# A state-space and feed-forward block: the first 512 tokens normalised and transposed in two halves, three tiles of gate and up matmuls at 256 columns

## The chip, the core and the metric

The kernel runs on one core of a Trainium2 chip. The time is device microseconds for one execution, the median of several runs; lower is better. TensorE does the matmuls, VectorE the elementwise work, ScalarE the activation functions and part of the copies out of PSUM, GpSimd a few small operations, and SyncE issues most DMAs. PSUM has eight banks of 128 x 512 fp32 here.

## The reference

The input x is 2048 tokens of 512 channels. It is normalised without weights, and two branches run on the result: a diagonal complex state-space layer with 512 states, and a gated feed-forward layer with 1376 hidden columns. The output is x plus both.

```python
xn = _layernorm(x, axis=-1)
# A: Lam_bar = exp(dt * Lam);  Bu = xn @ B_bar^T
#    h_t = Lam_bar * h_(t-1) + Bu_t;  y = 2 * Re(h @ C^T) + xn * Dskip
# B: (gelu(xn @ w_gate) * (xn @ w_up)) @ w_down
return x + A(xn) + B(xn)
```

Types are bf16, with fp32 sums in PSUM.

## The kernel before

The tokens are cut into four blocks of 512. Each block is normalised (LN), transposed so that channels lie on partitions (TR), and then used by three kinds of matmuls: gate and up (GU, 11 tiles of 128 hidden columns, the last of 96), the input of the state-space layer (BU), and the down and output matmuls of both branches into one bank (DN). Between BU and DN, VectorE turns the complex recurrence into real scans (CHAIN: multiplications with cosine and sine tables around 8 scans).

No engine's order is written by hand. Every operation is recorded with an engine, a function, an assumed duration and the buffers that it reads and writes (`S.op`, `S.dma`). `schedule` then walks through a model of the chip: TensorE and SyncE keep the order in which operations were recorded; VectorE, ScalarE and GpSimd take, of the operations whose inputs are recorded, the one with the earliest due time (worked back from the TensorE operation that needs it) if it can start within 150 ns of the earliest start, and otherwise fill the gap with work that fits. `emit` writes each engine's list in that order, with semaphore waits for what the buffers require. So the assumed durations decide the order, and the order is fixed when the chip runs. The planner knows no activation tables; the compiler puts a table load ahead of any ScalarE function that the loaded table does not hold.

The steps at the start, with their lines:

- Four DMAs load x of block 0, one per 128 tokens (L425). Three vectors of parameters (log_dt, Lambda_re, Lambda_im) follow on SyncE's queue (L409), then the first chunks of the gate and up weights (L421), Dskip, x of block 1 (L415), and so on. Weights come in three chunks of hidden columns, 0 to 512, 512 to 1024 and 1024 to 1376.
- 16 warm matmuls of 512 columns (L769) multiply the identity with the first x tile. Their result is not used.
- LN(0) on VectorE: statistics per 128 tokens (L563), aggregates (L564), casts and the addition of epsilon (L565 to L568). GpSimd takes the square root as a power of 0.5 (L569), VectorE the reciprocal (L570). Subtraction of the mean (L575) and multiplication (L583 on VectorE, L587 on ScalarE) are two operations per 128 tokens, with the buffer D1 between them.
- TR(0) on TensorE: two groups of eight 128 x 128 transposes (L609), each copied out of PSUM by ScalarE (L620) or VectorE (L616). Blocks 1 to 3 are transposed by DMA (L596) instead.
- GU(0): per tile, four matmuls for gate and four for up (L686) into two banks; ScalarE applies Gelu to the one (L690) and copies the other (L694); VectorE multiplies them (L696). Banks are dealt out in turn, eight of them (`next_bank`).
- The state-space parameters: Exp of log_dt (L482), Exp of its product with Lambda_re (L485), Sin (L493), a score of tiny VectorE operations (L483 to L510), and twelve diagonal matrices (L514). All Gelus wait for this Sin (`GATE`). Between GU(0)'s tiles from tile 4 on, prepB (L533, copied by L538) multiplies B with the diagonals.

In the later stages BU is L633 (copied by L637), DN is L730 and its result is added to x by L742.

Of the kernel before, what the change touches and what calls it, by code (L numbers as in the profile page):

```python
# [73 lines left out]
class Sched:  # L74
# [61 lines left out]
    def schedule(self, pe_start=12000.0):  # L136
# [40 lines left out]
        while nleft:  # L177
# [35 lines left out]
            if op.kind == "dma":  # L213
                free_at[e] = st + 60.0
                xfer = op.dur - 2000.0
                t0 = max(st, dma_pipe)
                dma_pipe = t0 + xfer
                op.finish = t0 + xfer + 2000.0
            else:
                op.finish = st + op.dur  # L220
                free_at[e] = op.finish
# [92 lines left out]
def build(nc, ins, out, dbg=None, stage=99, opts=None):  # L314
    dbg = dbg or {}
    opts = opts or {}
    with ExitStack() as es:
        E = es.enter_context
        S = Sched(nc, es)
        S.fence_slack = float(opts.get("fence_slack", FENCE_SLACK))  # L320
# [12 lines left out]
        FCH = [(0, 512), (512, 1024), (1024, F)]  # L333
# [9 lines left out]
        D1_all = A.alloc("D1", [4, D], BF16); D1 = ring(D1_all, "D1", 4)  # L343
# [13 lines left out]
        MB = A.alloc("MB", [NB, 4], BF16)  # L357
        NEGM = A.alloc("NEGM", [NB, 4], F32)
# [5 lines left out]
        blk = lambda buf, b, nm: A.sub(buf, "%s_%d" % (nm, b), b)  # L364
        MBb = [blk(MB, b, "MB") for b in range(NB)]; NEGMb = [blk(NEGM, b, "NEGM") for b in range(NB)]
        VBb = [blk(VB, b, "VB") for b in range(NB)]; SBQb = [blk(SBQ, b, "SBQ") for b in range(NB)]
        QBb = [blk(QB, b, "QB") for b in range(NB)]; RQb = [blk(RQ, b, "RQ") for b in range(NB)]
# [34 lines left out]
        if "DN" in dbg:  # L402
            DNB = A.alloc("DNB", [4, D], F32)
# [8 lines left out]
        do_ssm = stage >= 3  # L412

# [5 lines left out]
        def ld_w(W, Wc, src, ci):  # L419
            f0, f1 = FCH[ci]  # L420
            return S.dma(lambda e: e.dma_start(W.ap[:, :, f0:f1], src[:, f0:f1].rearrange("(k p) f -> p k f", p=128)),  # L421
                         512 * (f1 - f0) * 2, writes=[Wc[ci]], tag="ld_w")
# [3 lines left out]
        if do_ssm:  # L426
            for T_, nm in ((LDT, "A_log_dt"), (LRE, "A_Lambda_re"), (LIM, "A_Lambda_im")):
                S.dma(ld_param(T_, ins[nm]), 1024, writes=[T_], tag="ld_" + nm)
# [4 lines left out]
        if do_ssm:  # L433
            for c, nm in enumerate(("A_B_re", "A_B_im")):
                S.dma(lambda e, c=c, nm=nm: e.dma_start(BN.ap[:, c], ins[nm].rearrange("(s p) d -> p s d", p=128)),
                      512 * 1024, writes=[A.sub(BN, "BN%d" % c, c)], tag="ld_" + nm)
# [8 lines left out]
        XT_DMA = opts.get("xt_dma", (1, 2, 3))  # L445

        def load_CT():
            CTc = [A.sub(CT_all, "CTc%d" % c, c) for c in range(2)]
            for c, nm in enumerate(("A_C_re", "A_C_im")):
                S.dma(lambda e, c=c, nm=nm: e.dma_start_transpose(CTc[c].ap, ins[nm]),  # L450
                      opts.get("ct_bytes", 2.0) * 512 * 1024, writes=[CTc[c]], tag="tr_" + nm, fenced=True)
        wchunk = lambda ft: 0 if ft < 4 else (1 if ft < 8 else 2)
# [5 lines left out]

        V(lambda e: e.memset(HALF.ap, 0.5), D_TINY, [], [HALF], "half")
        POOL(lambda e: e.iota(IOT.ap, [[1, 128]], base=0, channel_multiplier=-1), 300, [], [IOT], "iota")  # L460
        V(lambda e: e.tensor_scalar(IDN.ap, IOT.ap, 0.0, None, ALU.is_equal), d_dve_ts4x(128), [IOT], [IDN], "ident")
        if do_ssm:
            POOL(lambda e: e.iota(IOTJ.ap, [[1, 512]], base=0, channel_multiplier=0), 600, [], [IOTJ], "iotj")
# [13 lines left out]
        last_table_op = None  # L477
        GATE = {"before_gelu": []}
        if do_ssm:
            (A_, TH, RRr, LBR, LBI, N1, TAa, TBb, DEN, RDEN, TC, TD, NRE, TE, TF, NIM, CR, CI) = range(18)  # L480
            pa = lambda i: PA[i].ap
            t1 = ACT(lambda e: e.activation(DTB.ap, LDT.ap, ACTF.Exp), d_act(4), [LDT], [DTB], "exp_dt")  # L482
            V(lambda e: e.tensor_tensor(pa(A_), DTB.ap, LRE.ap, ALU.mult), D_TINY, [DTB, LRE], [PA[A_]])  # L483
            V(lambda e: e.tensor_tensor(pa(TH), DTB.ap, LIM.ap, ALU.mult), D_TINY, [DTB, LIM], [PA[TH]])
            t2 = ACT(lambda e: e.activation(pa(RRr), pa(A_), ACTF.Exp), d_act(4), [PA[A_]], [PA[RRr]], "exp_a", after=[t1])  # L485
            w16 = lambda a, b_: W16.ap[:, a:b_]
            W16p = [A.sub(A.alloc("W16v", [4, 4], F32, at=W16.lo), "W16_%d" % i, i) for i in range(4)]
            V(lambda e: e.tensor_scalar(w16(0, 4), pa(TH), 1.0 / TWO_PI, None, ALU.mult), D_TINY, [PA[TH]], [W16p[0]])
            V(lambda e: e.tensor_scalar(w16(4, 8), pa(TH), 512.0 / TWO_PI, None, ALU.mult), D_TINY, [PA[TH]], [W16p[1]])
            V(lambda e: e.tensor_scalar(w16(8, 16), w16(0, 8), 0.25, None, ALU.add), D_TINY, W16p[0:2], W16p[2:4])  # L490
            V(lambda e: e.tensor_copy(KI.ap, W16.ap), D_TINY, W16p, [KI])
            V(lambda e: e.tensor_tensor(FRC.ap, W16.ap, KI.ap, ALU.subtract), D_TINY, W16p + [KI], [FRC])
            t3 = ACT(lambda e: e.activation(SC16.ap, FRC.ap, ACTF.Sin, scale=SIN_SCALE), d_act(16), [FRC], [SC16], "sin16", after=[t2])  # L493
            GATE = {"before_gelu": [t3]}
            sinT, sinP, cosT, cosP = (SC16.ap[:, 4 * i:4 * i + 4] for i in range(4))
            V(lambda e: e.tensor_tensor(pa(LBR), pa(RRr), cosT, ALU.mult), D_TINY, [PA[RRr], SC16], [PA[LBR]])
            V(lambda e: e.tensor_tensor(pa(LBI), pa(RRr), sinT, ALU.mult), D_TINY, [PA[RRr], SC16], [PA[LBI]])
            V(lambda e: e.tensor_scalar(pa(N1), pa(LBR), -1.0, None, ALU.add), D_TINY, [PA[LBR]], [PA[N1]])
            V(lambda e: e.tensor_tensor(pa(TAa), LRE.ap, LRE.ap, ALU.mult), D_TINY, [LRE], [PA[TAa]])
            V(lambda e: e.tensor_tensor(pa(TBb), LIM.ap, LIM.ap, ALU.mult), D_TINY, [LIM], [PA[TBb]])  # L500
            V(lambda e: e.tensor_tensor(pa(DEN), pa(TAa), pa(TBb), ALU.add), D_TINY, [PA[TAa], PA[TBb]], [PA[DEN]])
            V(lambda e: e.reciprocal(pa(RDEN), pa(DEN)), 150, [PA[DEN]], [PA[RDEN]])
            V(lambda e: e.tensor_tensor(pa(TC), pa(N1), LRE.ap, ALU.mult), D_TINY, [PA[N1], LRE], [PA[TC]])
            V(lambda e: e.tensor_tensor(pa(TD), pa(LBI), LIM.ap, ALU.mult), D_TINY, [PA[LBI], LIM], [PA[TD]])
            V(lambda e: e.tensor_tensor(pa(NRE), pa(TC), pa(TD), ALU.add), D_TINY, [PA[TC], PA[TD]], [PA[NRE]])
            V(lambda e: e.tensor_tensor(pa(TE), pa(LBI), LRE.ap, ALU.mult), D_TINY, [PA[LBI], LRE], [PA[TE]])
            V(lambda e: e.tensor_tensor(pa(TF), pa(N1), LIM.ap, ALU.mult), D_TINY, [PA[N1], LIM], [PA[TF]])
            V(lambda e: e.tensor_tensor(pa(NIM), pa(TE), pa(TF), ALU.subtract), D_TINY, [PA[TE], PA[TF]], [PA[NIM]])
# [244 lines left out]
        if do_ssm:  # L753
            PREP_holder()
# [115 lines left out]
```

## Time and profile before

| | before |
|---|---|
| median of 3 runs | 191.8 us (191.75 to 192.15) |
| span of the profiled execution | 190.1 us (the page gives no other time of it) |
| TensorE busy | 183.3 us, 96% of the span |
| VectorE busy | 152.9 us, 80% |
| ScalarE busy | 88.6 us, 47% |
| granted TensorE clock | 1.000 throughout |
| first warm matmul, first gate matmul | 2.90 us, 10.47 us after the start |

The span is measured from the first to the last instruction. The busy time of TensorE includes the modelled tails of pipelined matmuls. A line such as "L686" is a line of the kernel. In a view of waits or a timeline, the bracket at the end tells how long the engine was idle before the instruction, and what ended the idle time.

### The profile page before, as it was taken

The numbers are of one execution on the slowest core, as the hardware profiler recorded it, in microseconds if no ns is written. First come the engines' busy times: TensorE is split into PE (matmuls) and PEld (weight loads), VectorE is DVE, ScalarE is ACT, GpSimd is POOL, SyncE is SP. The second block draws the span as 40 slices with busy tenths as digits, with TensorE's granted clock in tenths as the row PEclk, the third lists the DMA queues.
The fourth block names the chain that finished last, engine by engine and source line by source line (L and its number), as shares of the span: only waits on it lengthen the run. The fifth ranks groups of instructions, "written<-read, shape, count | busy, mean of one in ns | idle before, by whom it ended". The sixth has DMA issues, their size and how long they took to land.

```text
span 190.1 us, 2549 instructions
## 1 busy us (share of the span) xinstructions
PE 183.3 (96%) x944; PEld 87.6 (46%) x944; DVE 152.9 (80%) x265; ACT 88.6 (47%) x149; POOL 5.0 (3%) x10
## 2 busy tenths in 40 slices
PE   3989999999999999999999999999999999999993
PEld 1434664444444444444444444444444444444451
DVE  5869887089999999999999989999999999411111
ACT  2297988899996473000567910017676304000000
POOL 1200200002000000000002000000000000000000
PEclk9999999999999999999999999999999999999999
DMA  4899212784422000000000221000000000100100
GB/s 111 212 349 347 49 28 55 245 276 112 110 55 55 3 0 0 28 28 31 28 2 0 54 48 41 28 33 22 0 3 0 0 0 0 55 31 32 51 28 29
DMA packets 22908, 12.26 MB, mean 64 GB/s; under 512 B 13328, under 2 KB 22896, under 8 KB 22896
## 3 DMA queue, kind: packets, MB, share of 16 engines
q1 hardware_dynamic: 22896, 12.10, 22.7%
q8 instruction: 7, 0.11, 0.2%
q14 instruction: 5, 0.04, 0.1%
HBM read 7.38 MB, written 2.10 MB: 50 GB/s over the span
## 4 chain that ended last, share of the span: by engine, by line
PE 96%; DMA 1%; DVE 1%; issue 0%; DVEq 0%
PE PS L686 40%; PE PS L730 36%; PE PS L633 15%; PE PS L769 3%; PE PS L533 2%; DMA arena<-in_A_x_dram 1%; PE PS L609 0%; DVE arena L616 0%; DVE arena L742 0%; DVEq L281 0%
## 5 line engine op out<-in xcount | busy, mean ns | idle before, releaser
L686 PE MATMUL PS<-arena 128*128 128x512 bf16 (+1 forms) x352 | 77.3, 379 | 0.9 <-DVE arena L616 0.9
L730 PE MATMUL PS<-arena 128*128 128x512 bf16 (+2 forms) x368 | 69.8, 351 | 0.0
L686 PEld LDWEIGHTS PS<-arena 128*128 128x128 bf16 (+1 forms) x352 | 35.0, 100 | 40.7 <-issue 1.0
L730 PEld LDWEIGHTS PS<-arena 128*128 128x128 bf16 (+1 forms) x368 | 33.3, 98 | 35.9
L690 ACT ACTIVATE arena<-PS 128x512 bf16<-128x512 f32 (+1 forms) x44 | 26.4, 599 | 35.1 <-PE PS L686 23.3
L657 DVE TENSOR_TENSOR_SCAN arena<-arena 128x512 bf16<-128x512 f32 x32 | 38.5, 1253 | 0.0
L694 ACT ACTIVATE arena<-PS 128x512 bf16<-128x512 f32 (+1 forms) x44 | 26.3, 597 | 6.7 <-PE PS L686 6.4
L742 DVE TENSOR_TENSOR arena<-PS,arena 128x512 bf16<-128x512 f32 x16 | 10.9, 685 | 21.4 <-PE PS L730 21.3
L633 PE MATMUL PS<-arena 128*128 128x512 bf16 x128 | 28.1, 379 | 0.0
L637 ACT ACTIVATE arena<-PS 128x512 bf16<-128x512 f32 x32 | 17.5, 618 | 22.4 <-PE PS L633 22.1
L696 DVE TENSOR_TENSOR arena<-arena 128x512 bf16<-128x512 bf16 (+1 forms) x44 | 17.6, 418 | 3.6 <-ACT arena L694 3.6
L633 PEld LDWEIGHTS PS<-arena 128*128 128x128 bf16 x128 | 12.5, 98 | 15.0
L563 DVE BATCH_NORM_STATS2 arena<-arena 128x6 f32<-128x512 bf16 x16 | 9.9, 679 | 1.2 <-DMA arena<-in_A_x_dram 1.2
L669 DVE TENSOR_TENSOR arena<-arena 128x4096 bf16<-128x4096 bf16 x4 | 9.1, 2286 | 0.0
L646 DVE TENSOR_TENSOR arena<-arena 128x4096 bf16<-128x4096 bf16 x4 | 9.1, 2285 | 0.0
L670 DVE TENSOR_TENSOR arena<-arena 128x4096 bf16<-128x4096 bf16 x4 | 9.1, 2286 | 0.0
L647 DVE TENSOR_TENSOR arena<-arena 128x4096 bf16<-128x4096 bf16 x4 | 9.1, 2284 | 0.0
L769 PE MATMUL PS<-arena 128*128 128x512 bf16 x16 | 5.8, 543 | 2.9 <-DMA arena<-in_A_x_dram 2.9
L587 ACT ACTIVATE arena<-arena 128x512 bf16<-128x512 bf16 x10 | 7.1, 721 | 1.6 <-DVE arena L570 1.6
L569 POOL TENSOR_TENSOR arena<-arena 128x4 bf16<-128x4 bf16 x4 | 4.0, 1010 | 98.6 <-DVE arena L565 98.6
L554 DVE SCALAR_TENSOR_TENSOR arena<-arena 128x2048 f32<-128x2048 f32 x1 | 2.3, 2292 | 4.5 <-ACT arena L551 4.5
L575 DVE TENSOR_SCALAR arena<-arena 128x512 bf16<-128x512 bf16 x16 | 5.0, 347 | 0.1
(70 smaller groups left out, 72.7 us busy)
## 6 DMA issues: line engine op xcount, KB each, us to landing
out_dram<-arena SPq DMA_DIRECT2D x16, 128.0 KB, 1.7
arena<-in_A_x_dram SPq DMA_DIRECT2D x3, 512.0 KB, 5.5
arena<-in_B_w_down_dram SPq DMA_DIRECT2D x1, 1280.0 KB, 7.5
arena<-in_B_w_gate_dram SPq DMA_DIRECT2D x2, 512.0 KB, 5.5
arena<-in_B_w_up_dram SPq DMA_DIRECT2D x2, 512.0 KB, 6.5
arena<-in_A_x_dram SPq DMA_DIRECT2D x4, 128.0 KB, 2.2
arena<-in_A_B_re_dram SPq DMA_DIRECT2D x1, 512.0 KB, 7.4
arena<-in_A_B_im_dram SPq DMA_DIRECT2D x1, 512.0 KB, 7.9
```

Source lines behind the costliest of these rows:

```text
L563: V(lambda e, tt=tt: e.bn_stats(ST[tt].ap, X[tt].ap), d_dve_1x(512), [X[tt]], [ST[tt]], "bnst")
L633: ins_ = e.matmul(PS[bank][:, :], BBT[c][dk].ap[:, 128 * s:128 * (s + 1)], XNT[b].ap[:, dk, :], start=(dk == 0), stop=(dk == KD - 1))
L637: ACT(lambda e, bank=bank, k3=k3, s=s, c=c: e.activation(SSc[k3][s][c].ap, PS[bank][:, :], ACTF.Copy), d_act(512), [BANK[bank]], [SSc[k3][ ...
L646: V(lambda e: e.tensor_tensor(TA.ap, ssb.ap, cos4, ALU.mult), d_dve_tt2x(4096), [ssb, COST], [TA], "pre_c")
L657: V(lambda e, g=g, rb=rb, init=init: e.tensor_tensor_scan(g.ap, rb, g.ap, init, ALU.mult, ALU.add), d_dve_scan(512), [g, PA[RRr]] + ([CARc ...
L686: ins_ = e.matmul(PS[bank][0:m, :], W.ap[:, dk, 128 * ft:128 * ft + m], XNT[b].ap[:, dk, :], start=(dk == 0), stop=(dk == KD - 1))
L690: GATE["last_gelu"] = ACT(lambda e, bg=bg, kk=kk, m=m: e.activation(GG[kk].ap[0:m, :], PS[bg][0:m, :], ACTF.Gelu_apprx_tanh), d_act(512), ...
L694: ACT(lambda e, bu=bu, kk=kk, m=m: e.activation(UPB[kk].ap[0:m, :], PS[bu][0:m, :], ACTF.Copy), d_act(512), [BANK[bu]], [UPB[kk]], "evU")
L696: V(lambda e, kk=kk, m=m, ft=ft, k2=k2: e.tensor_tensor(HTt[k2][ft].ap[0:m, :], GG[kk].ap[0:m, :], UPB[kk].ap[0:m, :], ALU.mult), d_dve_tt ...
L730: ins_ = e.matmul(o_, l_, r_, start=(n == 0), stop=(n == len(mms) - 1))
L742: V(lambda e, bank=bank, ko=ko, tt=tt: e.tensor_tensor(OUTB[ko].ap, PS[bank][:, :], X[tt].ap, ALU.add), d_dve_1x(512), [BANK[bank], X[tt]] ...
L769: ins_ = e.matmul(PS[wb][:, :], IDN.ap, X[0].ap, start=True, stop=True)
```

## The change

The change removes options that were not in use, and edits the start:

- The planner takes a DMA issue to occupy its queue for 500 ns instead of 60.
- The three parameter vectors are issued from ScalarE's queue. The weight chunks are cut at 384 and 896 instead of 512 and 1024.
- The warm matmuls, 13 instead of 16, read a buffer that VectorE sets to zero as its first operation, and no longer x and the identity.
- Normalisation of a 128-token tile is one VectorE operation that subtracts the mean and multiplies; the bf16 copy of the mean and its negative are gone. LN takes a list of the 128-token tiles, and for block 0 runs for tiles 0 and 1 and then for 2 and 3. In block 0 ScalarE takes the square root; elsewhere GpSimd does as before.
- Block 0 is transposed in halves of 256 tokens (TR0), four transposes per bank, one bank copied by ScalarE and one by VectorE for each half.
- Tiles 0, 1 and 2 of GU(0) are computed in halves: 256-column matmuls for the first half of the tokens of all three tiles, then for the second half. The second transposes stand ahead of the first halves of tile 2. Gelu and the copy follow on whole tiles. The six banks of the three tiles are taken together, and the second transposes take two more.

The core of the diff, with re-indented and otherwise unchanged lines left out:

```diff
             if op.kind == "dma":
-                free_at[e] = st + 60.0
+                free_at[e] = st + 500.0
...
-        FCH = [(0, 512), (512, 1024), (1024, F)]
+        FCH = [(0, 384), (384, 896), (896, F)]
...
+                S.dma(ld_param(T_, ins[nm]), 1024, writes=[T_], tag="ld_" + nm, queue="scalar")
...
+        V(lambda e: e.memset(WRM.ap, 0.0), 150, [], [WRM], "wrm")
...
+        def LN(b, js=range(4), on_act=False):
+            j0, j1 = js[0], js[-1] + 1
+            vb, sbq, qb, rq = (cols(t, b, j0, j1) for t in (VB, SBQ, QB, RQ))
...
+            if on_act:
+                ACT(lambda e: e.activation(qb.ap, sbq.ap, ACTF.Sqrt), d_act(4), [sbq], [qb], "sqrt")
+            else:
+                POOL(lambda e: e.tensor_tensor(qb.ap, sbq.ap, HALF.ap[:, 0:j1 - j0], ALU.pow), 1100, [sbq, HALF], [qb], "pow")
+            V(lambda e: e.reciprocal(rq.ap, qb.ap), 150, [qb], [rq], "rq")
+            for j in js:
+                tt = 4 * b + j
                 xs = XN[tt % 8]
+                V(lambda e, tt=tt, j=j, xs=xs: e.tensor_scalar(
+                    xs.ap, X[tt].ap, mv.ap[:, j - j0, 0:1], rq.ap[:, j - j0:j - j0 + 1], ALU.subtract, ALU.mult),
+                  d_dve_ts4x(512), [X[tt], mv, rq], [xs], "ln_n")
+
+        def TR0(h):
             for dp in range(KD // 2):
                 bank = next_bank()
                 pt = PS[bank].bitcast(BF16)
...
+                    for q in range(2):
+                        for j in range(2):
+                            ins_ = e.transpose(pt[:, 256 * q + 128 * j:256 * q + 128 * (j + 1)],
+                                               XN[2 * h + j].ap[:, 128 * (2 * dp + q):128 * (2 * dp + q + 1)], IDN.ap)
...
+                if dp == 0:
+                    ACT(lambda e, src=src, dst=dst: e.activation(dst, src, ACTF.Copy), d_act(512), [BANK[bank]], [tok], "evT")
                 else:
+                    V(lambda e, src=src, dst=dst: e.tensor_copy(dst, src), d_dve_1x(512), [BANK[bank]], [tok], "evT")
...
+        def GU(b, fts=None, halves=False):
...
+            if halves:
+                for ft in fts:
+                    banks[ft] = (next_bank(), next_bank())
+                for h in range(2):
+                    for ft in fts:
+                        if h == 0 and ft == fts[-1]:
+                            TR0(1)
+                        for (W, Wc, bank) in zip((WG, WU), (WGc, WUc), banks[ft]):
+                            mm(ft, W, Wc, bank, 256 * h, 256 * (h + 1), [XT0[h]])
...
+        nwarm = 13
...
+                ins_ = e.matmul(PS[wb][:, :], WRM.ap[:, 0:128], WRM.ap, start=True, stop=True)
...
-        LN(0); TR(0)
+        LN(0, [0, 1], True)
+        TR0(0)
+        LN(0, [2, 3], True)
+        GU(0, [0, 1, 2], halves=True)
         LN(1)
-        for ft in range(KF):
-            GU(0, [ft])
-            if ft >= opts.get("prep_from", 4):
+        for ft in range(2, KF):
+            if ft > 2:
+                GU(0, [ft])
+            if ft >= 4:
                 prep_some(2)
-            if ft == opts.get("tr1_at", 2):
+            if ft == 2:
                 TR(1)
                 late_loads()
```

## The prediction

> **What bounds the kernel now.** I read the chain that ended last first, because it says which engine the end hangs on.
>
> ```profile
> 0.74 2.11 DMA arena<-in_A_x_dram
> 2.90 5.80 PE PS L769 x16
> 8.71 0.91 PE PS L609 x16
> 9.64 0.70 DVE arena L616
> 10.47 8.79 PE PS L686 x40
> 187.21 0.69 DVE arena L742
> ```
>
> The columns are start, length, what. TensorE is 96% of the span. The view of waits gives it two idle times, 2.9 us before the warm matmuls (L769) and 0.9 us before the first gate matmul (L686). From 10.47 us it never waits. So work taken off VectorE or ScalarE later is worth nothing by itself; only the lead, the 10.47 us before the first gate matmul, can be shortened, and the stream must stay closed behind it. Next, the timeline of VectorE and ScalarE in the lead.
>
> ```profile
> 2.88 2.47 DVE L563 BATCH_NORM_STATS2 arena<-arena 128x6 f32<-128x512 bf16 x4 [1.22 <-DMA arena<-in_A_x_dram]
> 5.27 0.36 DVE L564 BATCH_NORM_AGGREGATE arena<-arena 128x2 f32<-128x6 f32 x4
> 5.66 0.17 DVE L567 CAST arena<-arena 128x4 bf16<-128x4 f32 x1
> 5.87 0.17 DVE L568 TENSOR_SCALAR arena<-arena 128x4 bf16<-128x4 bf16 x1
> 7.16 0.18 DVE L570 RECIPROCAL arena<-arena 128x4 f32<-128x4 bf16 x1
> 7.49 0.87 DVE L583 TENSOR_SCALAR arena<-arena 128x512 bf16<-128x512 bf16 x3
> 0.73 1.28 ACT L482 ACT_TABLE_LOAD   x1 [0.73 <-PEq L855]
> 5.60 0.20 ACT L482 ACTIVATE arena<-arena 128x4 bf16<-128x4 bf16 x1 [3.58 <-DMA arena<-in_A_log_dt_dram]
> 10.11 0.20 ACT L485 ACTIVATE arena<-arena 128x4 f32<-128x4 f32 x1
> 10.32 1.28 ACT L493 ACT_TABLE_LOAD   x1
> 11.62 0.22 ACT L493 ACTIVATE arena<-arena 128x16 f32<-128x16 f32 x1
> 11.85 1.28 ACT L690 ACT_TABLE_LOAD   x1
> 13.15 0.60 ACT L690 ACTIVATE arena<-PS 128x512 bf16<-128x512 f32 x1
> ```
>
> Two things count. Each new function on ScalarE (Exp, Sin, Gelu) has a table load of 1.28 us right before it; the load itself waits for no data (at 0.73 it ran long before L482's data came), only for ScalarE's earlier work. And the first Gelu comes at 13.15, harmless now: PSUM's eight banks are dealt out in turn (0 warm, 1-2 transposes, 3-8 tiles 0 to 2, 1-2 tile 3), so tile 4 is the first to need the bank that this Gelu empties, at 10.47 + 32 x 0.2158 = 17.4 us (a 512-column matmul is 18.99 us / 88 = 0.2158 us).
>
> Last, the stretches of the DMA engines:
>
> ```profile
> 4.00:4.50 0.50, 0.50 (x2) 0.15 (x1) 0.50 (x2) 0.00 (x0) 0.00 (x0) 1.00 0.26 7
> 5.00:5.50 0.50, 0.50 (x3) 0.21 (x2) 0.50 (x5) 0.00 (x0) 0.00 (x0) 1.00 0.20 1
> 7.50:8.00 0.50, 0.50 (x4) 0.26 (x3) 0.50 (x3) 0.50 (x1) 0.00 (x0) 1.00 1.05 334
> ```
>
> The last two columns are the engines' share and GB/s. Between 4 and 6 us, while the three parameter vectors pass through SP's queue, a quarter of the engines is busy and almost no bytes move; after that it is full at 350 GB/s. By issue and time to landing, gate chunk 0 lands at 4.17 + 4.7 = 8.9, up chunk 0 at 4.72 + 5.8 = 10.5.
>
> **The sum is made on** the span, 190.1 us; the runs' median is 191.8, so 1.7 us lie around it. I take them as unchanged. About 0.2%, 0.4 us, is what a measurement of this kernel can tell from no change.
>
> **The change, part by part.**
>
> *Edits with one answer.* The dropped options, D1, MB and NEGM are no time on the path. Fused normalisation: L514 (two operations, 128x128) takes 251 ns, L465 (one) 249 ns, so one 128x512 fused instruction costs the 350 ns of L575 or L583, and 22 of these on VectorE and 10 of 721 ns on ScalarE become 16 on VectorE. Behind block 0 that is off the path (TensorE never waits; the nearest wait is the first down matmul, at 72.9 us, with the scan's last operation done at 71.5): 0. The planner's 500 ns per DMA issue only moves order.
>
> *Queues.* Three issues of 0.43 to 0.51 us leave SP, so gate chunk 0 is issued at 2.6, not 4.17, behind the x tiles whose bytes end near 4.0. At 350 GB/s the new 384-column chunks (393 KB) take 1.12 us each: bytes end at 4.0 + 2.24 = 6.2, and up lands near 6.6 (the last x tile landed at 2.1 + 2.2 = 4.3, 0.3 after its bytes), by 8.0 if the vectors hold it up; it is needed at 8.0. Chunk 1 (former landings 13.6 and 15.05, earlier by the same 2 to 3 us) is needed from 15.5, B (18.05 before) at 19. All hidden. The issues go to ScalarE, where they delay only the Exp table (2.2 to 3.5 us), ahead of its data.
>
> *First half normalised.* Statistics 0 and 1 end at 2.88 + 2 x 0.62 + 0.05 = 4.15; aggregates, cast and add took 0.69 us after the last statistic with four aggregates, now about 0.6: 4.75. The planner's rule (lowest due time, waits up to 150 ns accepted) puts statistic 2 next, to 5.4. Sqrt on ScalarE is 0.2 us (L485's shape) instead of 1.01 us on GpSimd, but stands behind Exp of log_dt and a Sqrt table. If log_dt, now issued at 0.74, needs its 3.0 us again, Exp ends at 3.95, the table at 5.25, Sqrt at 5.45. Reciprocal to 5.65, two fused operations 0.1 later at 0.26 spacing: XN ready at T = 6.3.
>
> *Warm matmuls.* The memset is in no row: between L459's 0.06 us (128x4) and L461's 0.55, taken 0.2, as it is a plain write. Start 1.1 to 1.5. Now ten matmuls run at 0.427 us and the rest at 0.216, so 13 take 4.27 + 0.65 = 4.9 us and end by 6.4; all slow, 5.6 us, they would end by 7.1 and T0 would wait up to 0.7 us.
>
> *Transpose and copies.* Copy p0 on ScalarE starts 0.43 us after the first of four transposes (8.54 to 9.19 was 0.65 with eight), and takes 0.60 (L690's shape). Copy p1 on VectorE lies between 0.35 (L583) and 0.69 (L616, twice as wide); 0.38. It starts after statistic 3 and both transposes, T + 0.75. First gate matmul at T + 1.25 = 7.55 instead of 10.47.
>
> *256 columns.* Between rows of 128 (0.89 / 16 = 0.0556) and 512 columns a straight line gives 0.109 us, so 48 halves take 5.23 us against 24 x 0.2158 = 5.18: +0.05; the second transposes are inside the stream now, 0.45 us.
>
> *Second half.* VectorE then does aggregates, cast, add, reciprocal and two fused operations, with Sqrt between: about 1.9 us from T + 1.13, so T0 of half 1 starts at S = T + 3.05 = 9.35. TensorE's four half groups end at T + 3.0: no gap.
>
> *What is late next.* Tiles 0 to 2 hold banks 3 to 8 and the second transposes 1 and 2, so **tile 3** now waits for the first Gelu, one tile sooner. TensorE gets there after the second transposes (0.45), tile 2's first halves (8 x 0.109 = 0.87) and 24 second halves (2.62): S + 3.94. ScalarE's order, by the planner's due times, is Exp, Sqrt, copy, Sqrt, copy, Exp, Sin, Gelu: the second Exp follows the second half's copy, whose due time is about 2 us earlier. That copy ends at S + 1.03, and then come *three* loads, not two: 3 x 1.29 + 0.20 + 0.22 + 0.06 = 4.15, rounded up to 4.3 for the hand-overs, Gelu 0.60, hand-over 0.13 (10.34 to 10.47). Tile 3 starts at S + 6.1 = 15.45: a new stall of 2.1 us. Before, tile 3 began at 10.47 + 24 x 0.2158 = 15.65. Queued behind it on TensorE is all the rest of the kernel. Sin, too, is late, by 1.8 us (11.84 to about 13.6), and with it the twelve diagonals, done at 15.16 before and at 17 now; the first prepB needs them after tile 4, at 15.45 + 3.45 = 18.9: hidden. A wait of 2.1 us is longer than any behind the trace's warm matmuls (0.86, after which L686 ran at full rate); if the slow rate came back, ten matmuls at 0.21 more would cost 2.1 us; I take none, by that row, and count it with the slower cases. Everything behind tile 3 is the same stream. Sum: 15.45 - 15.65 = **-0.2 us**: 2.9 us won at the first matmul, 0.5 spent on transposes and halves, 2.1 handed to the new wait, 0.1 lost in the seams.
>
> The page "ScalarE: Activation LUTs" of the Trainium skill, section "Table sets: the hidden batching unit", says that exp and sqrt sit in different sets and that all calls of one set should be batched; this change alternates them. The page prices a switch at about 2.7 us with its drain, where every load here takes 1.28 and the next ACTIVATE starts 0.02 later. By the page's price (an estimate) the three loads would cost 4.1 us more and the change would lose about 4; the rows decide.
>
> "Trainium Kernel Development and Optimization", section "Key Constraints", says that DMAs issued from SP and ACT share the same 16 engines, so another queue saves only issue time. The 1 GB/s stretch agrees that issue is what was lost; by the rule the vectors can still slow the x tiles.
>
> **The rivals.**
>
> *Slower: the vectors on ScalarE's queue come late.* They now run beside the x tiles and Sqrt stands behind log_dt. It decides from a landing of 3.8 us on, and each us beyond moves T, S and tile 3 by one. For it: it landed at 5.6 before, and a quarter of the engines was busy with vectors for 2 us. Against: then it was issued 1.9 us later. Landing at 4.8 gives +0.8 us, 192.6; at 5.6, +1.6, 193.4.
>
> *Faster: the chain of tables does not bind.* If Exp of a is issued ahead of the second copy, its load falls into ScalarE's idle time, the chain shortens by 1.5 us and tile 3 starts at S + 4.6 = 13.95: -1.7 us, 190.1. With no stall, S + 3.94 = 13.3: -2.35, 189.45. Against: the due times above; for: the order comes of a greedy planner that I followed by hand, and it knows no table loads.
>
> **How the numbers follow.** Own forecast 0.42: 191.8 - 0.2 = 191.6, its own range 191.2 to 192.2 (T from 5.9 to 6.9), of which 0.05 lies below and 0.03 above the 0.4 us. Faster rival 0.31, slower rival 0.27. So faster 0.36, same 0.34, slower 0.30. The range cuts about 0.1 at each end: 189.8 to 192.9.
>
> **What would show it.** First gate matmul near 7.6; five table loads ahead of the first Gelu, three in a row after the second copy; a TensorE wait of about 2 us, ended by ScalarE's Gelu, at 13.4; tile 3 at 15.45; no wait after. Wrong: fewer loads in a row, that wait under 1 us, log_dt past 4 us, or a new wait behind tile 3.

## The result, and the profile after

The changed kernel takes 194.51 us in the median of 4 runs (192.8 to 195.03), the kernel before 191.98 beside it: a ratio of 1.0118, 95% interval 1.0074 to 1.0162. It is slower, and above the range's end of 192.9. Three of its four runs, the profiled one among them, have a mean granted clock of 0.989 to 0.991; the fourth kept full clock and took 192.8. That difference, 1.7 us, is the larger part of the loss. The profiled run's span is 192.5 us, 2.4 more than before.

The chain that ended last, in the changed kernel (L663 is the gate and up matmul, L580 the transpose, L474 Exp of a, L482 Sin, L686 Gelu, L609 BU):

```profile
3.08 5.84 DMA arena<-in_B_w_up_dram
...
8.96 1.49 PE PS L663 x12
10.44 0.24 PE PS L580 x4
...
14.36 1.28 ACT L686
...
15.65 0.61 ACT arena L686
...
16.40 5.30 PE PS L663 x16
...
35.63 13.81 PE PS L609 x64
```

Before, from 10.47 on the chain stayed on TensorE up to the last addition. Now it goes through the up weights' first chunk, the second transposes and ScalarE's tables, and the Gelu holds TensorE until 16.40. BU starts at 35.63; before it started at 33.20 (the chain of the kernel before, where L633 is BU):

```profile
33.20 13.81 PE PS L633 x64
```

So the whole loss of 2.4 us lies ahead of BU. TensorE's timeline at the two places that matter (the bracket is the idle time ahead):

```profile
8.09 0.60 PE L663 MATMUL PS<-arena 128*128 128x256 bf16 x4 [0.61 <-DVE arena L556]
16.40 5.30 PE L663 MATMUL PS<-arena 128*128 128x512 bf16 x16 [2.01 <-ACT arena L686]
```

The first gate matmul did come early, 8.09 instead of 10.47. (It needs VectorE's copy of the transposes, L590, which stands directly ahead of the L556 that the bracket names.) But 16 matmuls of 512 columns, 3.61 us at full clock, take 5.30 behind a wait of 2.01. The stretches say why; the third column from the end is the granted clock:

```profile
4.50:5.00 0.50, 0.50 (x2) 0.15 (x1) 0.47 (x4) 0.50 (x1) 0.00 (x0) 1.00 0.20 7
16.40:18.40 2.00, 2.00 (x6) 0.77 (x7) 2.00 (x11) 2.00 (x5) 0.00 (x0) 0.61 0.87 303
18.40:20.40 2.00, 2.00 (x6) 0.69 (x5) 2.00 (x4) 1.39 (x3) 0.00 (x0) 0.54 0.03 8
20.40:22.40 2.00, 2.00 (x23) 1.36 (x21) 1.50 (x9) 1.21 (x3) 0.67 (x1) 1.00 0.00 0
16.40:16.82 0.42, 0.42 (x2) 0.19 (x3) 0.42 (x4) 0.42 (x2) 0.00 (x0) 1.00 1.12 386
16.83:20.22 3.39, 3.39 (x9) 1.16 (x8) 3.39 (x11) 2.90 (x6) 0.00 (x0) 0.50 0.40 135
```

The stretches of 2 us blur it; the last two lines are cut where the clock changes. Two matmuls behind the wait it falls to exactly half, stays there for 3.4 us, and is full again. Half the rate for 3.4 us loses 1.7 us, which is 5.30 - 3.61, and makes the run's mean clock 1 - 1.7 / 192.5 = 0.991. (The first line is for the lead: with the vectors in flight the DMA engines are busy for a share of 0.20 and move 7 GB/s.) VectorE and ScalarE, where L555 is the statistic, L567 the fused normalisation, L588 the copy of the transposes:

```profile
4.05 0.69 DVE L555 BATCH_NORM_STATS2 arena<-arena 128x6 f32<-128x512 bf16 x1 [0.31 <-DMA arena<-in_A_x_dram]
6.07 0.74 DVE L567 TENSOR_SCALAR arena<-arena 128x512 bf16<-128x512 bf16 x2
10.70 0.60 ACT L588 ACTIVATE arena<-PS 128x512 bf16<-128x512 bf16 x1 [1.96 <-PE PS L580]
11.32 1.28 ACT L474 ACT_TABLE_LOAD   x1
12.83 1.28 ACT L482 ACT_TABLE_LOAD   x1
14.36 1.28 ACT L686 ACT_TABLE_LOAD   x1
15.65 0.60 ACT L686 ACTIVATE arena<-PS 128x512 bf16<-128x512 f32 x1
```

The second x tile came late and held VectorE for 0.31 us (before, the four statistics ran back to back), so the normalised half was ready at 6.81. Behind the second copy stand three table loads in a row.

### The profile page after: what moved, and what is told of

It reads as the page before. It is cut to its first block, busy times and chain, and to the rows that moved or that the text cites. A ratio compares the mean times of both kernels' runs of the same rounds, so it can differ in the third digit from the quotient of the medians.

```text
span 192.5 us, 2575 instructions
## 1 busy us (share of the span) xinstructions
PE 185.4 (96%) x965; PEld 89.8 (47%) x965; DVE 152.3 (79%) x256; ACT 86.9 (45%) x144; POOL 4.2 (2%) x9
## 3 DMA queue, kind: packets, MB, share of 16 engines
q10 hardware_dynamic: 1584, 0.00, 0.4%
## 4 chain that ended last, share of the span: by engine, by line
PE 91%; DMA 3%; issue 2%; ACT 1%; SPq 1%; DVE 0%; DVEq 0%
PE PS L663 39%; PE PS L715 36%; PE PS L609 14%; DMA arena<-in_B_w_up_dram 3%; PE PS L522 2%; SPq L419 1%; ACT L686 1%; DVE arena L720 0%; ACT arena L686 0%; SPq L415 0%; PE PS L580 0%; ACT arena L482 0%; ACT arena L474 0%; ACT L474 0%; DVEq L281 0%
## 5 line engine op out<-in xcount | busy, mean ns | idle before, releaser
L663 PE MATMUL PS<-arena 128*128 128x512 bf16 (+2 forms) x376 | 79.5, 371 | 2.9 <-ACT arena L686 2.0
L715 PE MATMUL PS<-arena 128*128 128x512 bf16 (+2 forms) x368 | 69.8, 352 | 0.0
L663 PEld LDWEIGHTS PS<-arena 128*128 128x128 bf16 (+1 forms) x376 | 37.6, 101 | 42.2 <-issue 4.2
L715 PEld LDWEIGHTS PS<-arena 128*128 128x128 bf16 (+1 forms) x368 | 33.3, 98 | 35.9
L686 ACT ACTIVATE arena<-PS 128x512 bf16<-128x512 f32 (+1 forms) x44 | 26.4, 599 | 38.7 <-PE PS L663 26.1
L633 DVE TENSOR_TENSOR_SCAN arena<-arena 128x512 bf16<-128x512 f32 x32 | 38.7, 1253 | 0.0
L609 PE MATMUL PS<-arena 128*128 128x512 bf16 x128 | 28.1, 380 | 0.0
L609 PEld LDWEIGHTS PS<-arena 128*128 128x128 bf16 x128 | 12.5, 98 | 15.1
L555 DVE BATCH_NORM_STATS2 arena<-arena 128x6 f32<-128x512 bf16 x16 | 10.3, 684 | 1.7 <-DMA arena<-in_A_x_dram 1.7
L567 DVE TENSOR_SCALAR arena<-arena 128x512 bf16<-128x512 bf16 x16 | 5.7, 410 | 0.6 <-DVE arena L563 0.5
L562 POOL TENSOR_TENSOR arena<-arena 128x4 bf16<-128x4 bf16 x3 | 3.2, 1077 | 100.9 <-DVE arena L558 100.9
L624 DVE TENSOR_TENSOR arena<-arena 128x2048 bf16<-128x2048 bf16 x4 | 4.9, 1221 | 0.1
L647 DVE TENSOR_TENSOR arena<-arena 128x2048 bf16<-128x2048 bf16 x4 | 4.9, 1223 | 0.1
```

Source lines behind the costliest of these rows:

```text
L555: V(lambda e, tt=tt: e.bn_stats(ST[tt].ap, X[tt].ap), d_dve_1x(512), [X[tt]], [ST[tt]], "bnst")
L609: ins_ = e.matmul(PS[bank][:, :], BBT[c][dk].ap[:, 128 * s:128 * (s + 1)], XNT[b].ap[:, dk, :], start=(dk == 0), stop=(dk == KD - 1))
L633: V(lambda e, g=g, rb=rb, init=init: e.tensor_tensor_scan(g.ap, rb, g.ap, init, ALU.mult, ALU.add), d_dve_scan(512), [g, PA[RRr]] + ([CARc ...
L663: ins_ = e.matmul(PS[bank][0:m, c0:c1], W.ap[:, dk, 128 * ft:128 * ft + m], XNT[b].ap[:, dk, c0:c1], start=(dk == 0), stop=(dk == KD - 1))
L686: GATE["last_gelu"] = ACT(lambda e, bg=bg, kk=kk, m=m: e.activation(GG[kk].ap[0:m, :], PS[bg][0:m, :], ACTF.Gelu_apprx_tanh), d_act(512), ...
L715: ins_ = e.matmul(o_, l_, r_, start=(n == 0), stop=(n == len(mms) - 1))
```

## The experiments

My theory after the result had two halves: tile 3 starts 0.75 us later than before (16.40 against 15.65), because the lead is late and three table loads follow it; and the wait ahead of it lets the clock fall, which costs another 1.7. Line numbers below are of the kernel named.

### Is the slow clock a result of the wait? `fill`

Nine matmuls of 512 columns (zeros into bank 1, the result unused) fill the time in which TensorE waits:

```diff
         GU(0, [0, 1, 2], halves=True)
+
+        def fkeep(e):
+            ins_ = None
+            for _ in range(9):
+                ins_ = e.matmul(PS[1][:, :], WRM.ap[:, 0:128], WRM.ap, start=True, stop=True)
+            return ins_
+        PE(fkeep, 10.0, [WRM], [BANK[1]], "warm")
```

> The changed kernel with nine more matmuls of 512 columns (zeros, result unused, 9 x 0.216 = 1.9 us) between the halves of tiles 0 to 2 and tile 3, so that TensorE works through its wait; tile 3 still waits for the first Gelu. Own theory (the slow clock of tiles 3 and 4 comes of the 2.0 us of idle time in front of them): tile 3 starts at 16.4 as before, its 16 matmuls and those of tile 4 take 0.216 us each instead of about 0.43, 1.7 to 1.9 us are won, 192.7 us. Rival (the clock falls for the thin load of the whole lead, 7 to 14 us, with its short matmuls and gaps): the 16 matmuls still take 5.3 us, 194.5 us.

Measured: 192.57 us (192.38 to 192.81, 6 runs), ratio to before 1.0032 [1.002, 1.0043]; no run below a clock of 0.998. TensorE's timeline in `fill`:

```profile
14.16 2.11 PE L750 MATMUL PS<-arena 128*128 128x512 bf16 x9
16.34 3.61 PE L663 MATMUL PS<-arena 128*128 128x512 bf16 x16
```

Tile 3 starts at the same time (16.34), and its matmuls are at full rate. So about 1.9 us of the median (194.51 less 192.57) came from TensorE standing idle, not from the work. What is left against before, 0.6 us, is near the 0.75 by which tile 3 is late.

### Is the wait the Gelu's? `banks`

```diff
-                bank = next_bank()
+                bank = next_bank() if h == 0 else 1 + dp
```

The second transposes reuse banks 1 and 2, and tile 3 gets two banks that nobody holds. The order on every engine is the same.

> The changed kernel with the second transposes in banks 1 and 2 by name and not dealt from the ring, so that tile 3 gets banks 1 and 2 and tile 4 is the first to wait for the first Gelu. Order and operations of every engine are the same. Own theory (tile 3 waits for the bank that the first Gelu empties, and the Gelu for three table loads): tile 3 starts at 14.4 without a wait, tile 4 waits 0.3 us at 16.1 and starts at 16.4, 1.0 us ahead of the kernel before, no slow clock: 191.0 us. Rival (tile 3 is late because of the transfers or the diagonals, or the clock falls in the lead): 194 us or more.

Measured: 190.71 us (190.52 to 190.77, 4 runs), ratio 0.9931 [0.9915, 0.9948]. One line of assignment turns the change from slower into faster than before. Tile 3 starts without a wait, and tile 4 now asks for the Gelu, almost in time (TensorE's timeline in `banks`):

```profile
16.15 1.90 PE L663 MATMUL PS<-arena 128*128 128x512 bf16 x8 [0.20 <-ACT arena L686]
```

### A shorter chain and a shorter wait: `pow`, `powwarm`, `copies`, `early`

`pow` takes the two square roots of block 0 on GpSimd, as before the change, which leaves two loads behind the second copy instead of three.

```diff
-        LN(0, [0, 1], True)
+        LN(0, [0, 1])
...
-        LN(0, [2, 3], True)
+        LN(0, [2, 3])
```

> The changed kernel with block 0's square root on GpSimd as in the other blocks (no Sqrt table, so Exp stays loaded and two loads go). Own theory: each half's root takes 0.9 us longer, but the first half groups wait for the up weights until 8.9 anyway and the second transposes start at about 10.3 as now; after the second copy come two loads, not three, so tile 3 starts at about 14.95 after a wait of 0.5 us, no slow clock: 191.3 us. Rival (the shorter root is what the change lives on, the loads are beside the path): the second transposes come 1 us later and the time rises to 195 us.

Measured: 191.56 us in the median (191.27 to 194.05, 10 runs), ratio 1.0004 [0.9969, 1.0039]. Six runs at full clock take 191.27 to 191.61, as expected; four take 193.05 to 194.05 at a mean clock of 0.982 to 0.991, which I did not expect. TensorE's timeline of the profiled run, at full clock:

```profile
7.49 0.62 PE L580 MATMUL PS<-arena 128*128 128x128 bf16 x8 [1.74 <-DVE arena L567]
15.06 3.61 PE L663 MATMUL PS<-arena 128*128 128x512 bf16 x16 [0.50 <-ACT arena L686]
```

The wait for the Gelu is down to 0.50, but TensorE was idle for 1.74 ahead of the transposes. The slower root on GpSimd is part of that: they start at 7.49 instead of 6.86. The rest is that the 13 warm matmuls took 4.56 us in this run instead of 5.63, so the gap is not the same in every run. `powwarm` is `pow` with 17 warm matmuls instead of 13:

> The kernel of pow with 17 warm matmuls instead of 13. Four of ten runs of pow took 1.7 to 2.7 us more at a clock of 0.98 to 0.99, though its wait for the Gelu is only 0.5 us; it idles 1.7 us ahead of the first transposes. Own theory (the clock falls on too much idle time within some microseconds, so filling that idle time keeps it up): all runs at 191.3 to 191.7 us with a clock of 1.0. Rival (it is the Gelu wait or chance, whatever precedes it): slow runs remain, some 2 in 5, at 193 us. If four warm matmuls more delay the transposes in some runs, those are 0.3 to 0.6 us slower.

Measured: 191.43 us (191.28 to 191.61, 7 runs), ratio 0.9969 [0.9958, 0.998], all runs at a clock of 0.998 or more; the gap is 1.12 now. If the four runs that lost clock fell anywhere among these 17 by chance, all four would be runs of `pow` about 9 times in 100, and `powwarm` ran on another chip. So the gap is the likely cause here, not a shown one. No profile shows one of these four; the lowest of their mean clocks, 0.982, is about what two stretches of 3.4 us at half rate would make (an estimate).

`copies` moves the second half's other copy from ScalarE to VectorE, so that Exp of a need not wait behind it:

```diff
-                if dp == 0:
+                if dp == 0 and h == 0:
```

> The changed kernel with both copies of the second transposes on VectorE, so that ScalarE has nothing between the second Sqrt (8.7) and the Exp of a. Own theory: the three loads start at 8.7 instead of 11.3 and run while ScalarE would be idle; the first Gelu ends by 13.9, tile 3 starts at 14.4 without a wait and without a slow clock, 1.2 us ahead of the kernel before: 190.8 us. Rival (the loads cost wherever they stand, or VectorE's second copy delays the second halves by its 0.4 us and more): 191.5 us or more.

Measured: 191.6 us (191.45 to 191.85, 10 runs), ratio 0.9975 [0.9964, 0.9986]. The wait shrank to 1.0 and no run lost clock, but I had expected 190.8. ScalarE's timeline in `copies` shows why:

```profile
10.21 1.28 ACT L474 ACT_TABLE_LOAD   x1 [1.40 <-DVE arena L472]
```

ScalarE was idle from 8.80 to 10.21 with nothing left ahead, and the load still did not start: it waited for L472, the product that Exp of a reads. My statement that a load waits for no data fails here. Exp and Sin carry two waits each, one for their data and one for the fixed order (`after`). In the trace of `copies` the Exp itself waits for the semaphore that ScalarE's own operations raise, which is the order; the wait for L472 stands at its load, as the bracket says. `early` is `copies` without the fixed order:

```diff
-..., "exp_a", after=[t1])
+..., "exp_a")
...
-..., "sin16", after=[t2])
+..., "sin16")
```

> The kernel of copies without the two ordering edges between Exp of log_dt, Exp of a and Sin (the data give the order anyway), which leaves each of them a single wait. In copies the table load of Exp of a started only at 10.21, with that instruction's data, not at 8.8. Own theory (where an instruction has two waits, the first one stands ahead of its table load; with one wait the load runs as soon as ScalarE is free): Exp load at 8.8, Sin load at 10.4, first Gelu at 13.7, tile 3 at 14.4 with no wait or under 0.2 us, 190.7 us. Rival (the loads wait for something else, such as the writes of the operand): the load stays at 10.2, 191.6 us.

Measured: 190.45 us (190.36 to 190.59, 4 runs), ratio 0.9917 [0.9904, 0.993]. ScalarE's timeline in `early`:

```profile
8.81 1.28 ACT L474 ACT_TABLE_LOAD   x1
```

The load starts as soon as ScalarE is free, and in the trace the wait for VectorE's semaphore is now at the Exp itself. The first Gelu comes at 13.37 instead of 14.55, and tile 3 at 14.32 behind a gap of 0.15. So the rival "the chain of tables does not bind" was a real version of this kernel, three small edits away.

### Why was the lead late? `novec`, `dsk`, `hold`, `holdv`, `bed`

All of these start from `banks`, where nothing behind the lead covers a gain up. `novec` does not load the three parameter vectors; GpSimd writes constants in their place.

> The kernel of banks, with the three parameter vectors not loaded but filled with constants by GpSimd (the state-space branch then has constant parameters; this part of the computation is changed); the order on VectorE, ScalarE and TensorE is that of banks. Own theory (the 2-byte pieces of these vectors hold up the x tiles and the first weights, whichever queue issues them): the second x tile is there by 3.5 instead of 4.1, up chunk 0 before 7 instead of 8.9, the first gate matmul comes at 7.6 instead of 8.25, the second transposes at 9.45 instead of 10.1, tile 4 0.6 us sooner: 190.1 us. Rival (x and weights are as fast as SyncE's issue lets them be): no transfer moves by over 0.2 us, 190.5 us or more.

Measured: 190.19 us (189.77 to 190.61, 4 runs), ratio 0.9903 [0.9884, 0.9921]. VectorE's and TensorE's timelines in `novec`:

```profile
2.81 1.29 DVE L555 BATCH_NORM_STATS2 arena<-arena 128x6 f32<-128x512 bf16 x2 [1.05 <-DMA arena<-in_A_x_dram]
8.59 1.48 PE L663 MATMUL PS<-arena 128*128 128x256 bf16 x12 [0.56 <-DMA arena<-in_B_w_up_dram]
```

The second statistic follows at once, the transposes start at 6.21 and the first gate matmul at 7.44: the vectors were what held up the x tiles. But the up chunk still comes late, at 8.55, and TensorE waits 0.56 for it. What holds it? `dsk` is `novec` with Dskip, a fourth vector of 2-byte pieces, loaded behind all weights:

> The kernel novec (no parameter vectors loaded, tile 3 in the banks of the second transposes), and the load of Dskip, also made of 2-byte pieces, moved from right behind the first weight chunks to the end of SyncE's list of weight loads. Nothing else is moved on any engine. Own theory, that pieces of 2 bytes hold up whatever else is in flight: the first up chunk lands near 7.0 instead of 8.58 us, TensorE no longer waits for it, the second transposes start near 9.3 instead of 9.91, 189.6 us. Rival, that the up chunk is late because of the volume in flight ahead of it (x tiles, gate chunk): it lands at 8.6 again, 190.2 us as novec.

Measured: 190.0 us (189.76 to 190.37, 4 runs), ratio 0.9901 [0.9882, 0.9919]. The up chunk lands at 8.3. That is 0.25 earlier, nearer to the 8.6 of the rival than to my 7.0, and the time is that of `novec` within the spread. `hold` also keeps back the loads behind the up chunk (the planner gets one more dependency, of x of block 1 on the first reciprocal):

> The kernel dsk (no parameter vectors, Dskip last, tile 3 in the banks of the second transposes); the loads behind the first up chunk (second 512 tokens, second weight chunks, B) are held on SyncE until the first half's reciprocal is done, issued from about 5.4 instead of 3.63 us. Same order on every engine. Own theory, that loads issued later share the 16 DMA engines with the ones ahead of them (in dsk 1.76 MB had moved by the time the 1.31 MB of x tiles and first chunks were complete): the up chunk lands at 7.4 instead of 8.3 us. Rival, that the engines serve loads in the order of issue: it lands at 8.3 again. As TensorE did not wait for it in dsk, 190.0 us by both, within 0.4.

Measured: 189.92 us (189.82 to 190.45, 3 runs; 0.9872 [0.985, 0.9894] against a before of 192.51 on that chip). The chunk lands at 8.0: 0.3 earlier, a third of the step that my theory asked for, and less than profiles of one arrangement differ (8.5 in `pow`, 8.9 in the changed kernel, with the same loads in the same order). That later loads share the engines with it is not shown by this. The same hold with the vectors in place:

> The kernel banks (vectors on ScalarE's queue as in the changed kernel), with the same hold of the loads behind the first up chunk until the first half's reciprocal. Same order on every engine. Own theory, that with vectors the engines are lost to them first (a share of 0.2 at 7 to 15 GB/s from 4.0 to 5.0 us) and later loads take only 0.13 MB ahead of the up chunk: it lands 0.3 to 0.4 us earlier, at 8.4 instead of 8.78, 190.6 us. Rival, that the later loads are the whole delay: it lands at 7.4 as without vectors, second transposes at 9.6, 190.2 us.

Measured: 190.6 us (190.53 to 190.66, 3 runs), 0.99 [0.9881, 0.992]; the chunk lands at 8.7 instead of 8.8 in `banks`. The rival, that the later loads are the whole delay, falls; my own 8.4 was missed too, though the time was as expected. `bed` keeps the vectors, moves Dskip back and takes out the fixed order of Exp and Sin:

> The kernel banks (the changed kernel with tile 3 in the banks of the second transposes) with the fixed order of Exp and Sin taken out, so that their table loads carry no second wait, and Dskip's load moved to the end of the weight loads; the vectors stay on ScalarE's queue. All of the reference is computed. TensorE's and ScalarE's orders are those of banks. Own theory: the wait of 0.2 us before tile 4 goes, and the up chunk lands earlier than 8.9: second transposes at 9.9, 190.2 us. Rival: the up chunk's landing has nothing to do with Dskip, second transposes at 10.1, 190.5 us.

Measured: 190.86 us (190.78 to 190.91, 4 runs), ratio 0.9943 [0.9928, 0.9958]. The chunk lands at 8.94 and the second transposes start at 10.30; the rival's mechanism is right, Dskip is not the cause while the vectors are in flight, and the time is even 0.36 above its 190.5. The fixed order makes no difference either, since ScalarE is busy with the copy until 11.33.

### Everything at once: `best` and `best2`

`best` is `banks` with the vectors on SyncE's queue behind the first weight chunks, and Exp of log_dt ordered behind both square roots, so that Sqrt, Exp, Sin and Gelu are each loaded once:

> The kernel of banks with the parameter vectors on SyncE's queue behind the first weight chunks, and Exp of log_dt ordered behind the second Sqrt, so that ScalarE loads Sqrt, Exp, Sin and Gelu once each. Own theory (x, then weights, then vectors is the order in which they are needed): up chunk 0 lands near 6.9, first gate matmul 7.6, second transposes 9.5, tile 3 at 13.6, first Gelu done by 15.2, no wait above 0.2 us after the first gate matmul; tile 4 at 15.35 against 17.38 in the kernel before: 189.9 us. Rival (the vectors, landing at 8 to 9 now, hold up VectorE or the first Gelu): tile 4 waits 1 us or more, 190.9 us or more.

Measured: 190.5 us (190.16 to 190.88, 4 runs), ratio 0.9919 [0.9903, 0.9936]. The up chunk lands at 7.8 and nobody waits for it or for a Gelu, but VectorE's timeline in `best` shows a new wait:

```profile
8.58 0.16 DVE L492 TENSOR_TENSOR arena<-arena 128x4 f32<-128x4 bf16 x1 [0.63 <-DMA arena<-in_A_Lambda_re_dram]
8.97 0.16 DVE L493 TENSOR_TENSOR arena<-arena 128x4 f32<-128x4 bf16 x1 [0.22 <-DMA arena<-in_A_Lambda_im_dram]
```

The planner had put two tiny squares of Lambda ahead of the second half's reciprocal, and they wait 0.85 us for the vectors that are now late: the rival's mechanism, though it is the second transposes that wait and not tile 4. `best2` orders them behind the normalisation and moves Dskip back:

> The kernel best (tile 3 in the banks of the second transposes, vectors on SyncE's queue behind the first weights, Exp ordered behind both Sqrt), with Dskip's load moved to the end of the weight loads, and the two VectorE operations that square the Lambda vectors ordered behind the last normalisation of the first 512 tokens. Own theory: VectorE no longer waits for a vector ahead of the second half's reciprocal; the second transposes start at 9.35 instead of 10.23, tile 3 near 13.4, the first Gelu is done by 15.2, no wait for it: 189.7 us. Rival: the vectors come so late that Sin, and with it the first Gelu, is what tile 4 waits for: 190.3 us or more.

Measured: 190.0 us (189.8 to 190.1, 4 runs), ratio 0.9898 [0.9883, 0.9912]: the lowest ratio of the kernels that compute the whole reference, though the interval of `holdv` (0.99, on another chip) covers it. TensorE's timeline in `best2`:

```profile
9.48 0.61 PE L587 MATMUL PS<-arena 128*128 128x128 bf16 x8
11.21 6.23 PE L670 MATMUL PS<-arena 128*128 128x256 bf16 x40 [0.24 <-DVE arena L487]
```

The second transposes start at 9.48 (9.35 expected), the up chunk lands at 7.4, and the only wait behind them is 0.24: VectorE's copy of the second half stands behind four parameter operations, which start at 10.09, and begins at 10.64. With the 0.13 of the transposes that is the 0.3 us by which my 189.7 was missed.

### The rest of the normalisation: `fusedb`

The kernel before, with the fused operation in blocks 1 to 3 only:

```diff
+                if b > 0:
+                    V(lambda e, tt=tt, b=b, j=j, xs=xs: e.tensor_scalar(
+                        xs.ap, X[tt].ap, MV[b].ap[:, j, 0:1], RQb[b].ap[:, j:j + 1], ALU.subtract, ALU.mult),
+                      d_dve_ts4x(512), [X[tt], MV[b], RQb[b]], [xs], "ln_n")
+                    continue
```

> The kernel before, with one VectorE operation for each normalised tile in the second, third and fourth 512 tokens only; the first 512 tokens, the order on TensorE and the first 21 groups on VectorE stay as they are. Own theory: this part of the change is off the path, as TensorE never waits there: 192.0 us, within 0.3. Rival: the ten freed ScalarE operations of 721 ns and the six of VectorE bring evictions forward and something of the change's time comes from there: below 191.6 us.

Measured: 192.22 us (191.86 to 192.66, 10 runs) beside 191.88, ratio 1.001 [1.0, 1.002]. No gain, as priced: the ScalarE operations of about 0.72 us that it removes were off the path. (They are nine, not ten: the tenth belongs to the first 512 tokens.) The traces say it more sharply than the medians. From the first gate matmul to the end of the last matmul it is 176.6 us in both kernels:

```profile
10.47 8.79 PE PS L686 x40
152.44 34.64 PE PS L730 x184
11.24 8.79 PE PS L691 x40
153.21 34.65 PE PS L735 x184
```

The first two lines are of the kernel before, the last two of `fusedb`. The 0.77 us between their starts comes almost wholly from the warm matmuls, 5.80 us in the one profile and 6.53 in the other.

## Why the prediction was wrong

**The step that failed: "if the slow rate came back, ten matmuls at 0.21 more would cost 2.1 us; I take none".** The wait was forecast rightly (2.1 us, measured 2.01), the price nearly (2.1, measured 5.30 - 3.61 = 1.7 us, eight slow matmuls and not ten), and the chance wrongly: the clock fell in three of four runs. The row I chose, a wait of 0.88 us behind the warm matmuls, was the nearest in the trace of before and still too short to speak for 2.1. `fill` settles it. This step alone would have put the forecast of 191.6 at 193.3, outside the range; the start of the second transposes, below, would have put it at 192.5, inside.

Page "TensorE: Matmul & The Clock Gate" of the Trainium skill, section "Why this matters for your kernels", asks for no idle gaps over about 3 us, and its Part 1 describes a free-running idle window of about 3.4 us. Here one gap of 2.01 us sufficed in three runs of four, and gaps of 1.0 us (`copies`, 10 runs) and 1.12 us (`powwarm`, 7 runs) did no harm; the measurement decides. The half rate lasted 3.4 us here, the length that the page gives for its window. That the loss changes from run to run fits a window which runs freely, but no run here shows where a window begins.

**The term that was mis-sized: S, the start of the second transposes, 10.28 instead of 9.35.** By parts: XN of the first half was ready at 6.81 instead of 6.3, as the second x tile came late; from there to the first gate matmul 1.28 against 1.25, as priced; then 0.27 us of wait for the up chunk, which landed at 8.92 and not by 6.6 (8.0 at worst); the rest, about 0.1, is in seams. The sum of the bytes assumed that the weights follow the x tiles without a gap, that the vectors cost them nothing, and that loads are served in order. The landings of the up chunk, one profile each (the issue at 3.08 and the time to landing, which some views give to 0.1 us):

| kernel | in flight beside or ahead of it | up chunk lands, us |
|---|---|---|
| after, `fill`, `banks`, `copies`, `early`, `pow`, `powwarm` | vectors, Dskip, later loads | 8.9, 8.9, 8.8, 8.8, 8.7, 8.5, 8.9 |
| `bed` | vectors, later loads | 8.9 |
| `holdv` | vectors, Dskip | 8.7 |
| `novec` | Dskip, later loads | 8.6 |
| `dsk` | later loads | 8.3 |
| `hold` | later loads held back | 8.0 |
| `best`, `best2` | vectors issued behind it | 7.8, 7.4 |

The kernels of the first row have the same loads in the same order and differ by 0.4. So only this is clear: 8.5 to 8.9 with the vectors ahead, 8.0 to 8.6 without them, 7.4 to 7.8 where they and the bulk loads come behind. For the second x tile it is plainer. It lands 2.8 to 2.9 us after its issue in all nine kernels with the vectors on ScalarE's queue, and 2.0 to 2.1 us in `novec`, `hold`, `best` and `best2`; `dsk`, with 2.6, is the exception that nothing here explains. How the chunk's delay divides between vectors, Dskip, the later loads and the start of a load stays open: even in `hold` the engines move only 37 GB/s from 4.0 to 4.5 us, although the gate chunk was issued at 2.60. For the time it matters little. In `dsk`, where TensorE no longer waits for the chunk, the second transposes start only 0.06 us earlier than in `novec` (9.85 against 9.91). There the late x tile held VectorE (timeline of `dsk`), so that the first half was normalised at 6.56 instead of 6.15, and the slow warm matmuls held TensorE a little longer:

```profile
3.82 0.69 DVE L555 BATCH_NORM_STATS2 arena<-arena 128x6 f32<-128x512 bf16 x1 [0.26 <-DMA arena<-in_A_x_dram]
```

**What held.** The chain behind S: predicted S + 6.1, measured 16.40 - 10.28 = 6.12, with five table loads ahead of the first Gelu and three in a row, in the order that the due times gave. Diagonals, prepB and B's load stayed hidden; no wait came behind tile 3. The 256-column matmuls cost 0.109 us each (in `dsk` 16 of them fill the 1.74 us from 8.11 to 9.85). The fused operation takes 410 ns, not 350, and that cost nothing behind block 0 (`fusedb`). With tile 3 at 16.40 and full clock the sum would have said 191.98 + 0.75 = 192.7; the undisturbed run took 192.8, `fill` 192.57.

**The rivals.** *Slower, vectors late:* no. Data of log_dt was there at 3.7 us. The vectors did harm, but by holding up the second x tile (by 0.7 to 0.9 us against `novec`, `hold`, `best` and `best2`) and with it, by a part that stays open, the weights. The rule quoted in the prediction, that queues share the engines, was the right warning, and I left its term at zero. *Faster, chain not binding:* not in the changed kernel, but its mechanism is that of `early` (190.45), and `banks` (190.71) takes the wait away by another road; I had put 189.45 to 190.1. The statement that a load waits for no data holds at 0.73 and 2.36 us and fails in `copies`.

## What to carry to other kernels

Price a new wait on TensorE twice: for its length, and for the matmuls at half rate behind it; a wait of 2 us is already long enough to need work that fills it, or another bank that takes it away. When an early stage is pulled forward, count the banks first: who holds the one that the next tile asks for, and until when. And put loads of tiny strided vectors behind the bytes that the first matmuls need; then look at which queue inherits the wait for them.

## What the runs showed of the hardware

- The granted clock falls to half for 3.4 us behind a TensorE wait of 2.01 us in the profiled run, and the mean clock shows a loss of that size in 3 of 4 runs. In `pow`, with a gap of 1.74 in its profile, 4 of 10 runs lost clock; in the 27 runs of `fill`, `copies`, `powwarm` and `early` together, with gaps up to 1.21 in theirs, none did. The longest gap is not the only reading: the three gaps ahead of tile 3 add up to 2.89 us in the changed kernel and 2.85 in `pow`, against 2.44, 2.30 and 1.97 in `powwarm`, `copies` and `early`. No run separates one long gap from the sum, and where the loss begins was not tried.
- While three loads of 1 KB in 2-byte pieces were in flight, the DMA engines of the changed kernel were at a share of 0.2 and moved 7 to 15 GB/s (4.0 to 5.0 us; in `banks`, with the same loads, 0.47 and 56 to 101), and the second x tile, on another queue, landed 0.7 to 0.9 us later than in four of the five kernels without them beside it. Page "DMA: Bandwidth & Descriptors" of the Trainium skill, section "Rules for kernel authors", says that a non-contiguous last dimension becomes one descriptor per element; the trace agrees: ScalarE's queue carried 1584 packets for the 1536 elements of these three vectors.
- A table load can be held by the data wait of the operation behind it: 10.21 with two waits (`copies`), 8.81 with one (`early`).
- Whether the warm matmuls reach full rate differs between profiled runs: 13 of them took 5.63 us in the changed kernel, 4.56 in `pow`, 4.40 in `novec`. Those that take 0.43 us each stand in stretches whose granted clock reads 1.00, so that column does not show this half rate.
